# Output row of a decode kernel: four column groups of 112 columns on four partitions, one VectorE copy, a store from four partitions

## The chip, the cores and the metric

One core of a Trainium2 chip. The metric is the device time of one execution in microseconds (us); most executions of one kernel agree within about 0.9 us here, so medians of 3 to 9 runs are quoted. Before the change the median was 1276.21 us. Times inside an execution are counted from the start of its span; the span is about 1.3 us shorter than the timed execution.

## The reference, cut to what matters

One token goes through grouped attention over a cache of 65,536 positions and through a small gated feed-forward net; a gate mixes the two. Both halves end in a projection onto the same row of 448 numbers, so the kernel adds them in one accumulator.

```
q = x @ wq                                   # 448 -> 16 heads x 256
p = softmax(q k^T / 16);  o = p v            # k_cache, v_cache: 8 x 65536 x 256, bf16
a = o.reshape(1, 4096) @ wo                  # 4096 -> 448
h = relu(x @ W_gate) * (x @ W_up)            # 448 -> 1792
b = h @ W_down                               # 1792 -> 448
out = g * a + (1 - g) * b                    # row of 448, bf16 (896 B)
```

The two caches are 537 MB and have to be read once.

## The kernel before: what the change and the argument touch

The accumulator row lies in one PSUM tensor (the memory that the matmuls write), `A_ps` of 128 x 512 f32, as two halves of 224 columns on partitions 0 and 32. `proj` adds one contraction tile of 128 rows to it: two matmuls with a stationary operand of one column, in two column groups of the array. They run side by side: in the tail of the trace the two start 4 to 5 ns apart, and in a row the next pair starts 187 ns later, at a granted clock of 0.50.

```
D2 = D // 2                                   # 224
def proj(e, lhsT, rhs, start, stop):
    for g in range(2):
        ins = e.matmul(A_ps[32*g:32*g+1, 0:D2], lhsT, rhs[:, g*D2:(g+1)*D2], start=start, stop=stop,
                       skip_group_check=True, tile_position=(0, 32*g))
    return ins
# [...] down projection (ahead of the loop): 14 contraction tiles
def f_dn(e):
    for ft in range(FT):
        ins = proj(e, hT[:, ft:ft+1], wd_sb[:, ft, :], ft == 0, False)
# [...] output projection (after the loop): 8 heads x 4 tiles; weights come in five transfers, wo0 to wo4
def f_wo4(e, h=h):
    for s in range(4):
        ins = proj(e, attnT[:, h*4+s:h*4+s+1], wo4[:, h, s, :], False, False)
# [...] the end
fin_o = P_sb[0:1, 0:D]
f0 = op("dv", T_END, lambda e: e.tensor_copy(fin_o[:, 0:D2], A_ps[0:1, 0:D2]), [fin])
f1 = op("ac", T_END, lambda e: e.copy(fin_o[:, D2:D], A_ps[32:33, 0:D2]), [fin])
f2 = dma("sp", T_END + 1, "out", lambda e: e.dma_start(out[0, :, :], fin_o), [f0, f1])
```

TensorE's program has three pieces: code ahead of the loop over heads, the loop, and code after it (called the tail code here).

## Time and profile before

| | before |
|---|---|
| median of 3 runs | 1276.21 us (1276.04 to 1276.6) |
| span of the profiled execution | 1275.2 us |
| DMA traffic | 549 MB at 431 GB/s |
| matmuls into `A_ps` | 28 (down) + 64 (output), 224 columns each |

The kernel is bound by its transfers: the DMA engines are busy from first to last slice, no compute engine over half the time. Queue q8 carried 7 transfers of kind "instruction". It is 0.0% of the traffic.

The end of the chain of waits that ended last (start, duration, what):

```profile
1246.84 0.43 SPq L582
1247.28 0.04 issue
1247.32 23.46 DMA ring<-in_A_wo_dram
1270.78 0.04 issue
1270.82 0.91 PE A_ps L391 x8
1271.73 0.20 PE M_ps L426 x4
1271.93 1.67 PE A_ps L391 x15
1273.59 0.02 issue
1273.62 0.38 DVE P_sb L619
```

The timeline of the last 5 us (start, duration, engine, line, operation, output<-input, count, idle time before it and its releaser), then the wait of the store's queue:

```profile
1270.82 0.91 PE L391 MATMUL A_ps<-ring,attnT 128*1 128x224 bf16 x8 [0.73 <-DMA ring<-in_A_wo_dram]
...
1271.91 1.66 PE L391 MATMUL A_ps<-ring,attnT 128*1 128x224 bf16 x16
...
1273.04 0.09 PEld L391 LDWEIGHTS A_ps<-ring,attnT 128*1 128x1 bf16 x4 [0.29 <-DMA ring<-in_A_wo_dram]
1273.62 0.34 ACT L620 CAST P_sb<-A_ps 1x224 bf16<-1x224 f32 x1 [58.59 <-PE A_ps L391]
1273.62 0.38 DVE L619 CAST P_sb<-A_ps 1x224 bf16<-1x224 f32 x1 [1.49 <-PE A_ps L391]
1274.05 0.32 SPq L621 DMA_DIRECT2D out_dram<-P_sb  x1
```

```profile
SPq L644 <- DMA out_dram<-P_sb: 0.8, 1, 0.8
```

Read from the bottom: 0.8 us to the store's landing, 0.32 us to issue it, two copies side by side (the longer 0.38 us), and before them the last four matmuls, which a weight transfer released at 1273.04 us. Only this tail is not hidden under transfers. The matmul clock there is half speed, by windows (window, length, busy time of each engine and count, PEclk, DMA share, GB/s):

```profile
1271.00:1272.00 1.00, 1.00 (x14) 0.50 (x12) 0.04 (x1) 0.00 (x0) 0.00 (x0) 0.50 0.33 124
```

### The profile page before, as it was taken

How to read it: one execution, taken by the hardware profiler on the slowest of the kernel's cores; microseconds unless marked ns; L12 is line 12 of the kernel's file. 1: busy time of each engine (PE TensorE's matmuls, PEld its weight loads, DVE VectorE, ACT ScalarE, POOL GpSimd, SP SyncE). 2: the span in 40 equal slices, each digit the busy share in tenths (PEclk: the TensorE clock that was granted, in tenths of full speed). 3: DMA queues.
4: the chain of work that ended last, by engine and by line, in shares of the span. 5: the costliest groups of instructions: out<-in, count | busy, mean ns of one | idle time of the engine just before them, and what ended most of it. 6: DMA issues, size and time to landing. Idle time of an engine off the chain costs nothing. (4 is left out here: it accounts for less than half of the span.)

```text
span 1275.2 us, 10054 instructions
## 1 busy us (share of the span) xinstructions
PE 420.1 (33%) x4572; PEld 160.9 (13%) x4572; DVE 625.3 (49%) x240; ACT 63.3 (5%) x124; POOL 4.6 (0%) x21
## 2 busy tenths in 40 slices
PE   2423432334123432225331243322333324233235
PEld 1201110111001210012110111100111101011012
DVE  2697633465433655434555444555434655335600
ACT  0001000010000100001000010000100001000000
POOL 1000000000000000000000000000000000000000
PEclk8566666656566565666665666656666656666567
DMA  9999999999999999999999999999999999999998
GB/s 402 451 423 426 440 428 442 432 430 432 436 438 434 430 430 436 432 438 434 432 432 436 434 432 436 430 434 434 436 434 432 430 438 432 436 436 428 423 438 356
DMA packets 12050, 549.19 MB, mean 431 GB/s; under 512 B 1283, under 2 KB 1798, under 8 KB 3078
## 3 DMA queue, kind: packets, MB, share of 16 engines
q1 hardware_dynamic: 12034, 549.03, 99.7%
q8 instruction: 7, 0.11, 0.0%
q14 instruction: 5, 0.04, 0.0%
q10 hardware_dynamic: 4, 0.00, 0.0%
HBM read 549.03 MB, written 0.00 MB: 431 GB/s over the span
## 5 line engine op out<-in xcount | busy, mean ns | idle before, releaser
L369 DVE STREAM_TRANSPOSE ring<-ring 128x8192 uint32<-128x8192 uint32 x64 | 553.9, 8691 | 402.5 <-DMA ring<-in_A_k_cache_dram 402.5
L380 PE MATMUL ST<-ring,xc 128*16 128x512 bf16 x2048 | 223.8, 610 | 738.8 <-PEq L86 737.7
L380 PEld LDWEIGHTS ST<-ring,xc 128*16 128x16 bf16 x2048 | 68.4, 120 | 879.5 <-issue 877.3
L411 PE MATMUL O<-ring,ptp 128*4 128x512 bf16 x2048 | 150.2, 456 | 36.4 <-PEq L86 24.0
L521 ACT ACTIVATE P_sb<-ST,nmb 128x512 bf16<-128x512 f32 x32 | 45.2, 1412 | 1102.8 <-DVE nmb L519 1102.8
L519 DVE TENSOR_REDUCE nmb<-ST 128x1 f32<-128x512 f32 x32 | 22.0, 689 | 118.3 <-PE ST L380 118.3
L411 PEld LDWEIGHTS O<-ring,ptp 128*4 128x4 bf16 x2048 | 57.0, 100 | 129.7 <-issue 81.8
L421 DVE CAST o_sb<-O 128x512 bf16<-128x512 f32 x8 | 5.5, 691 | 77.5 <-PE O L411 77.5
L540 DVE TENSOR_TENSOR P_sb<-P_sb,hs 128x1024 bf16<-128x1024 bf16 x16 | 18.9, 1221 | 9.6 <-ACT hs L534 9.6
L545 PE MATMUL PT<-identb,P_sb 128*128 128x128 bf16 x128 | 16.2, 306 | 16.8 <-PEq L86 15.8
L545 PEld LDWEIGHTS PT<-identb,P_sb 128*128 128x128 bf16 x128 | 12.4, 138 | 19.2 <-issue 19.2
L554 ACT COPY ptp<-PT 128x256 bf16<-128x256 bf16 x32 | 10.3, 375 | 23.9 <-PE PT L545 23.9
L343 PE MATMUL QN<-ring,P_sb 128*128 128x512 bf16 x32 | 8.4, 429 | 3.9 <-DMA ring<-in_A_wq_dram 3.9
L521 ACT ACTIVATION_READ_ACCUMULATOR P_sb<-ST,nmb 128x1 f32 x32 | 8.4, 262 | 0.0
L478 PE MATMUL QN<-ring,xT 128*1 128x448 bf16 x16 | 1.7, 566 | 18.1 <-DMA ring<-in_B_W_up_dram 18.1
L433 PE MATMUL M_ps<-emat,o_sb 128*64 128x1 bf16 x112 | 4.5, 199 | 6.6 <-PEq L86 6.6
L458 DVE STREAM_TRANSPOSE scr<-P_sb 128x256 uint32<-128x256 uint32 x1 | 0.4, 445 | 12.7 <-ACT P_sb L457 12.7
L530 PE MATMUL M_ps<-identf,hs 128*2 128x128 f32 x8 | 2.6, 321 | 11.1 <-PEq L86 11.1
L440 DVE TENSOR_SCALAR attnT<-M_ps,hs 64x4 bf16<-64x4 f32 x14 | 3.1, 220 | 6.3 <-PE M_ps L433 6.2
L566 DVE RECIPROCAL hs<-M_ps 128x2 f32<-128x2 f32 x8 | 1.4, 170 | 8.3 <-PE M_ps L565 8.3
L433 PEld LDWEIGHTS M_ps<-emat,o_sb 128*64 128x64 bf16 x112 | 4.1, 154 | 9.9 <-issue 9.9
L391 PE MATMUL A_ps<-ring,attnT 128*1 128x224 bf16 x64 | 4.7, 305 | 1.3 <-DMA ring<-in_A_wo_dram 0.7
(80 smaller groups left out, 70.4 us busy)
## 6 DMA issues: line engine op xcount, KB each, us to landing
ring<-in_A_v_cache_dram SPq DMA_DIRECT2D x1, 4096.0 KB, 48.1
ring<-in_A_wq_dram SPq DMA_DIRECT2D x1, 3072.0 KB, 10.5
ring<-in_A_wo_dram SPq DMA_DIRECT2D x1, 2240.0 KB, 38.9
ring<-in_A_v_cache_dram SPq DMA_DIRECT2D x1, 2048.0 KB, 19.1
ring<-in_B_W_down_dram SPq DMA_DIRECT2D x1, 1568.0 KB, 22.8
ring<-in_B_W_gate_dram SPq DMA_DIRECT2D x1, 1344.0 KB, 32.6
ring<-in_B_W_up_dram SPq DMA_DIRECT2D x1, 1344.0 KB, 35.5
ring<-in_A_v_cache_dram SPq DMA_DIRECT2D x1, 1024.0 KB, 21.2
```

Source lines behind the costliest of these rows:

```text
L343: ins = e.matmul(QN_ps, xw3[:, k_, 31 - h:159 - h], rhs, start=(h == 0 and kt == 0), stop=(h == H - 1 and kt == R3))
L369: return lambda e: e.transpose(v, v)
L380: ins = e.matmul(bank[32 * w:32 * w + 16, :], xc[:, x0:x0 + 16], ktv[sl][:, u0:u0 + 16, c, :, r_], start=(b == 0 and c == 0 and r_ == 0), ...
L391: ins = e.matmul(A_ps[32 * g:32 * g + 1, 0:D2], lhsT, rhs[:, g * D2:(g + 1) * D2], start=start, stop=stop, skip_group_check=True, tile_pos ...
L411: ins = e.matmul(OP[32 * g:32 * g + 4, :], ptp[:, col:col + 13:4], ring[sl][:, base + k * 512:base + (k + 1) * 512], start=(a == 0 and k < ...
L421: o1 = op("dv", tn, lambda e: e.tensor_copy(o_sb[:], OP[:]), [pv[n], last.get(("otr", h - 1))])
L433: ins = e.matmul(T_ps[64 * q:64 * q + 64, s:s + 1], o_sb[:, par * 256 + s:par * 256 + 256:4], emat[:, 2 * par + q:2 * par + q + 1], start= ...
L519: smax[n] = op("dv", tk + 22, lambda e, n=n, NM=NM, t_=t_: e.tensor_reduce(NM[:, t_:t_ + 1], ST[n % 2][:], AX.X, ALU.max, negate=True), [q ...
L521: aexp[n] = op("ac", tk + 23, lambda e, n=n, t_=t_, NM=NM, RS=RS: e.activation(P_sb[:, t_:2048:4], ST[n % 2][:], ACTF.Exp, bias=NM[:, t_:t ...
L540: rsc = op("dv", tt, lambda e, X=X, pb=pb: e.tensor_tensor(pb, pb, X[:, 12:16].unsqueeze(1).to_broadcast([128, 256, 4]), ALU.mult), [h7, a ...
L545: ins = e.transpose(PT[rd][:, s * 128:(s + 1) * 128], P_sb[:, (rd * 8 + s) * 128:(rd * 8 + s + 1) * 128], identb[:, :])
L554: ins = e.copy(dst, src)
```

## The change

Its intent is to shorten the tail: four column groups at once instead of two, a copy half as wide on one engine, one wait fewer before the store. The new memset keeps the unused partitions of the copied block defined.

```
-        fin_o = P_sb[0:1, 0:D]
+        fin_o = P_sb[:, 0:D // 4]
 [...]
-        for i, tt in enumerate([ST[0], ST[1], OP]):
+        for i, tt in enumerate([ST[0], ST[1], OP, A_ps]):
             c_ps.append(op("dv", 0.04 + i * 0.001, lambda e, tt=tt: e.memset(tt[:], 0.0)))
 [...]
-        D2 = D // 2
+        D4 = D // 4
         def proj(e, lhsT, rhs, start, stop):
-            for g in range(2):
-                ins = e.matmul(A_ps[32 * g:32 * g + 1, 0:D2], lhsT, rhs[:, g * D2:(g + 1) * D2], ...
+            for g in range(4):
+                ins = e.matmul(A_ps[32 * g:32 * g + 1, 0:D4], lhsT, rhs[:, g * D4:(g + 1) * D4], ...
 [...]
-        f0 = op("dv", T_END, lambda e: e.tensor_copy(fin_o[:, 0:D2], A_ps[0:1, 0:D2]), [fin])
-        f1 = op("ac", T_END, lambda e: e.copy(fin_o[:, D2:D], A_ps[32:33, 0:D2]), [fin])
-        f2 = dma("sp", T_END + 1, "out", lambda e: e.dma_start(out[0, :, :], fin_o), [f0, f1])
+        f0 = op("dv", T_END, lambda e: e.tensor_copy(fin_o, A_ps[:, 0:D4]), [fin])
+        f2 = dma("sp", T_END + 1, "out", lambda e: e.dma_start(
+            out[0, :, :].rearrange("o (g d) -> (o g) d", g=4), fin_o[0:128:32, :]), [f0])
```

More of the change, by code (lines that the diff above doesn't have):

```diff
@@ L384, in f_qk @@
             return f
-        D2 = D // 2
+        D4 = D // 4
+        assert D % 4 == 0
         def proj(e, lhsT, rhs, start, stop):
-            for g in range(2):
-                ins = e.matmul(A_ps[32 * g:32 * g + 1, 0:D2], lhsT, rhs[:, g * D2:(g + 1) * D2], start=start, stop=stop,
+            for g in range(4):
+                ins = e.matmul(A_ps[32 * g:32 * g + 1, 0:D4], lhsT, rhs[:, g * D4:(g + 1) * D4], start=start, stop=stop,
                                skip_group_check=True, tile_position=(0, 32 * g))
@@ L503, in f_dn @@
                     return ins
-                l_["dn"] = op("pe", tg + 12.2, f_dn, [l_["hT"], a3])
+                l_["dn"] = op("pe", tg + 12.2, f_dn, [l_["hT"], a3, c_ps[3]])
                 assert tg + 12.2 < tL["k", 0] + 20
```

## The prediction

> **What bounds the kernel now.** HBM traffic. On the page the DMA engines are busy 9 tenths or more in all but the last of 40 slices, the hardware queue takes 99.7% of 16 engines' span, 431 GB/s for 549 MB. DVE is busy 49%, PE 33%. The chain of waits that ended last is one transfer of projection weights (23.5 us, to 1270.8 us) and about 4.4 us of tail. Only what lies in this tail, or what empties the DMA queue earlier, can move the time.
>
> **What the change touches.**
> 1. The projections into A_ps (down and output): each pair of matmuls over 224 columns becomes four over 112; by tile 28 + 64 matmuls become 56 + 128.
> 2. One more PSUM memset at the start on DVE (the present ones take 485 ns each).
> 3. The last copy: one DVE cast of 112 columns over 128 partitions instead of a DVE (379 ns) and an ACT cast (336 ns) of 224 columns side by side.
> 4. The store: four runs of 224 B from four partitions instead of one of 896 B.
>
> **Costs from the trace.** In the tail the granted clock is 0.50 (windows of 1 us, 1271 to 1275 us), and projection pairs start 187 ns apart (timeline, sixteen matmuls in 1.66 us): 224 columns at half clock, two column groups side by side. Four groups of 112 stream together in 93 ns, if issue keeps up. It should: the 16 one-column matmuls of the attention transpose, with their weight loads, take 0.65 us, 198 ns of it the last one's own duration: at most 30 ns each, 120 ns for four. [...] So about 100 to 120 ns per four instead of 187 per pair, and about 0.09 us less in the last matmul's own duration.
>
> On the critical path: the last weight piece lands near 1273.0 us and only four matmuls (0.53 us, to 1273.57) follow. They become eight in 0.35 to 0.4 us: gain 0.15 us. The down projection at 53 us gets about 1 us shorter, and the transfer that waits for it is issued earlier, but the queue isn't empty there: no gain. The first five heads' output projection at 1246 us (full clock, 52 ns a matmul) lies under transfers.
>
> Copy: 512 columns take 691 ns, 224 take 379, so 1.08 ns a column; 112 take about 260 ns: gain 0.12 us. ACT's copy wasn't the longer one.
>
> Memset: 0.49 us at about 4.1 us; the query projection waits for weights until 11.7 us, its DVE input is ready at 5.4 us: hidden.
>
> Store: today 0.32 us issue, 0.8 us to landing. [...] I allow 0 to 0.2 us more.
>
> **Sum:** -0.15 - 0.12 + 0.1, about -0.2 us: 1276.0 us, inside the spread of before's runs (0.56 us). Range 1275.0 to 1277.0. Faster by over 2%: 0.5%; within 2%: 98.5%; slower: 1%.
>
> **What would show it.** A_ps matmuls in the tail in fours within 100 to 120 ns at clock 0.50, own durations near 165 ns instead of 259; under 0.5 us from the last weight landing to the copy; copy near 260 ns; store wait 0.8 to 1.0 us; DMA share still 99%; query projection still from 11.7 us.
>
> **What would make it wrong.** If weight load plus matmul issue at 50 ns, four take 200 ns and the tail gains nothing. If four small stores take over 0.5 us more. If the earlier issue at 53 us reorders transfers so that a piece lands late at the end.

The sum: it came to -0.15 (matmuls) - 0.12 (copy) + 0.1 (store) = -0.17, about -0.2 us. But what is left for "about 100 to 120 ns per four" is the 93 ns of streaming and the at most 30 ns a matmul of the trace, and "0 to 0.2 us more" for the store, the source of the +0.1, is a guess of mine, drawn from no run.

## More of the kernel before

From the page of the kernel before (busy times; busy tenths of the DMA engines in 40 slices; DMA queues with packets, MB and share of 16 engines):

```profile
span 1275.2 us, 10054 instructions
PE 420.1 (33%) x4572; PEld 160.9 (13%) x4572; DVE 625.3 (49%) x240; ACT 63.3 (5%) x124; POOL 4.6 (0%) x21
...
DMA  9999999999999999999999999999999999999998
...
q1 hardware_dynamic: 12034, 549.03, 99.7%
q8 instruction: 7, 0.11, 0.0%
q14 instruction: 5, 0.04, 0.0%
```

The tail code is placed *ahead* of the loop in memory and skipped the first time:

```
pl.emit("pe", pe[:heads[0][0]], nc.tensor)                   # ahead of the loop
with nc.tensor.Fori(0, 2) as part:
    with nc.tensor.If_eq(part.val.handles[0], 1):
        pl.emit("pe", pe[end:], nc.tensor)                   # tail code, run in the second round
    with nc.tensor.If_eq(part.val.handles[0], 0):
        pl.emit_loop(H + 1, span, nc.tensor, go)             # the loop, run in the first round
```

## The result, and the profile after

| | before | after |
|---|---|---|
| median of 6 runs each | 1276.22 us (1275.99 to 1276.6) | 1277.36 us (1277.31 to 1277.63) |
| ratio after/before | | 1.0009 (95%: 0.9996 to 1.0022) |

Ratios are the mean time of one kernel's fast runs over that of the other's of the same rounds, so not quite the ratio of the medians. Executions over 1.5% slower than the fastest of the same kernel are left out of the means. The median lies 0.36 us above the top of the range, and by the medians the change cost 1.14 us where I had expected a gain of 0.2. No run of the one kernel overlaps the other's, so 0.1% or not, something systematic happened.

The same lines of the page after:

```profile
span 1276.0 us, 10237 instructions
PE 413.8 (32%) x4664; PEld 157.6 (12%) x4664; DVE 625.8 (49%) x241; ACT 63.1 (5%) x123; POOL 4.5 (0%) x21
...
DMA  9999999999999999999999999999999999999998
...
q1 hardware_dynamic: 12040, 549.03, 99.6%
q8 instruction: 9, 0.15, 0.0%
q14 instruction: 5, 0.04, 0.0%
```

The program has 92 more matmuls and 92 more weight loads, and q8 carried 9 instruction transfers instead of 7. The end of the chain, the timeline and the store's wait:

```profile
1249.67 23.92 DMA ring<-in_A_wo_dram
1273.59 0.04 issue
1273.64 0.38 PE A_ps L392 x8
1274.02 0.02 issue
1274.04 0.28 DVE P_sb L620
```

```profile
1272.50 0.94 PE L392 MATMUL A_ps<-ring,attnT 128*1 128x112 bf16 x24 [0.48 <-DMA ring<-in_A_wo_dram]
...
1273.64 0.36 PE L392 MATMUL A_ps<-ring,attnT 128*1 128x112 bf16 x8 [0.20 <-DMA ring<-in_A_wo_dram]
1274.04 0.28 DVE L620 CAST P_sb<-A_ps 128x112 bf16<-128x112 f32 x1 [1.82 <-PE A_ps L392]
1274.34 0.64 SPq L621 DMA_DIRECT2D out_dram<-P_sb  x1
```

```profile
SPq L645 <- DMA out_dram<-P_sb: 1.0, 1, 1.0
```

Walk the tail in both timelines. The last weights release TensorE at 1273.04 us before and 1273.64 after: **+0.6**. From there to the copy's start 0.58 and 0.40: **-0.18**. From the copy's start to the store's issue 0.43 and 0.30: **-0.13**. Issue 0.32 and 0.64, landing 0.8 and 1.0: **+0.5**. The sum is +0.8 us, the difference of the two spans. The profiled execution of before was one of the longer runs (1276.48 us, 0.26 above the median), so the typical difference of the landing is larger than 0.6, as the runs below show.

So the two gains came as predicted, the store cost more than I had allowed, and there is a term that the prediction didn't have at all: the last weights land later.

### The profile page after: what moved, and what is told of

It is laid out like the page before. It is cut to its first block, busy times and chain, and to the rows that moved or that the text cites. A ratio compares the mean times of both kernels' runs of the same rounds, so it can differ in the third digit from the quotient of the medians.

```text
span 1276.0 us, 10237 instructions
## 1 busy us (share of the span) xinstructions
PE 413.8 (32%) x4664; PEld 157.6 (12%) x4664; DVE 625.8 (49%) x241; ACT 63.1 (5%) x123; POOL 4.5 (0%) x21
## 5 line engine op out<-in xcount | busy, mean ns | idle before, releaser
L412 PE MATMUL O<-ring,ptp 128*4 128x512 bf16 x2048 | 147.4, 450 | 36.2 <-PEq L86 23.7
L533 PE MATMUL M_ps<-mx,nselT 2*128 2x1 f32 x16 | 3.4, 279 | 4.1 <-PEq L86 4.1
```

The costliest lines, as they stand in the source:

```text
L412: ins = e.matmul(OP[32 * g:32 * g + 4, :], ptp[:, col:col + 13:4], ring[sl][:, base + k * 512:base + (k + 1) * 512], start=(a == 0 and k < ...
L533: h5 = mop("pe", T + 15, lambda e, h=h: e.matmul(NMR_ps, nselT[0:2, :], mx2[0:2, 0:1], start=True, stop=True), [h4, l_["ns"]])
```

## The experiments

**Theory A**, which the runs below are to test: TensorE's longer program no longer fits in what it can hold. Near the end it fetches two 16 KB blocks of instructions, through the same DMA engines that carry the data. Each fetch delays one of the 16 engines, and the last weights are complete only when the slowest engine has delivered. The trace has q8's packets, of 16,384 B each, with their times: before, all 7 lie between 54 and 107 us. After, 7 lie there and two more start at 1251.86 us (lasting 1.06 us) and 1263.24 us (1.09 us). I take q8 to be TensorE's because its packets change where only TensorE's program does: in the five padded kernels below there are 7 to 11 of them, while q14 keeps its 5. **Rival B.** The last group of transfers was issued 0.65 us later (1246.18 us against 1245.52), because TensorE happened to be at half clock for longer just before (PEclk from 1240 to 1244 us 0.50, in before 0.59): late issue, late landing. **Rival C.** The new shapes or the memset.

Here is the evidence that ties A to the landing, from the trace. Every large transfer has 16 landings (wo4's lie from 1270.44 to 1273.00 us before), as many as the page counts DMA engines. The landings carry no engine number, only times. That each is the landing of one engine is my reading, and "an engine" below means one of the 16 in this reading; that they keep their distances from transfer to transfer, as shown below, agrees with it. The last three landings of three transfers:

```
                                             before                      after
the cache tile (8 MB) due at 1260       1258.86 1259.12 1259.72     1259.19 1259.33 1259.77
the 2 MB piece after it                 1263.75 1264.02 1264.61     1264.09 1264.21 1264.67
wo4, the fifth transfer of weights      1272.16 1272.40 1273.00     1272.61 1273.02 1273.59
```

The slowest engine is within 0.06 us of before until 1264.7 us and then 0.6 us later: just the transfers behind the fetch of 1263.24 us. All 16 landings, compared from the 2 MB piece to the transfer after it, show how: fifteen move on by the same 2.48 us to within 0.04, and one falls behind them by about 1.5 us, more than the 1.09 us that the fetch itself lasted. That engine was not the last before (it would have landed at about 1266.2 us and landed at 1267.71), and from there on it is the last. The fetch of 1251.86 us also set one engine back by 1.5 us, but one that was 2.5 us ahead of the last, and cost nothing. In each experiment below, "last landing" is the last of wo4's 16.

### TensorE's program made longer, nothing else: pad_before

The kernel before plus 92 one-column matmuls into an unused corner of `A_ps`, 28 beside the down projection and 64 in the tail code, at a time when transfers hide them.

```
+        def dummy(e, lhsT, rhs, n):
+            for _ in range(n):
+                ins = e.matmul(A_ps[64:65, 256:257], lhsT, rhs[:, 0:1], start=True, stop=True, ..., tile_position=(0, 64))
 [...] in f_dn:   + ins = dummy(e, hT[:, ft:ft + 1], wd_sb[:, ft, :], 2)
 [...] in f_wo4:  + if h < 4: ins = dummy(e, attnT[:, ...], wo4[:, h, s, :], 4)
```

> The kernel before plus 92 one-column matmuls that nobody reads (28 beside the down projection, 64 under the transfers at 1246 us), so that TensorE's program is as long as after the change; copy and store as before. Theory A (the longer program makes TensorE fetch two more 16 KB blocks of instructions near the end, and each fetch takes a slice of one DMA engine, so the last weights land later): the instruction queue shows 9 transfers instead of 7, two of them after 1250 us, last weight landing about 0.6 us later, time +0.5 to +1.0 us on the kernel before. Rival B (the final transfers are issued 0.65 us later because the half-clock phase fell differently): no change beyond 0.3 us. Rival C (the shapes of the matmuls or the extra memset): no change.

Measured: 1277.15 us (1276.98 to 1277.38) against 1276.00 (1275.84 to 1276.07) for before on the same chip; ratio 1.0009. Its queue line, and its end with before's own copy and store:

```profile
q8 instruction: 9, 0.15, 0.0%
```

```profile
1274.21 0.38 DVE L628 CAST P_sb<-A_ps 1x224 bf16<-1x224 f32 x1 [1.45 <-PE A_ps L391]
1274.64 0.32 SPq L630 DMA_DIRECT2D out_dram<-P_sb  x1
```

Fetches at 1249.51 and 1255.91 us, last landing at 1273.59 us. Instructions that compute nothing cost 1.15 us, as much as the whole change (+1.14) and a little more than expected. Rivals B and C are not needed for it. In this trace one engine lands the cache tile at 1260.31 us, 1.2 us behind the second slowest, and stays 1.2 us behind to the end: a lag handed on unchanged for 13 us. TensorE itself also stands for 2.3 us up to 1251.86 us here, which I read as a wait for instructions, but that is over 8 us before the cache tile lands.

### The change with the program made short again: trim_after

Half of the down projection's tiles and four heads' output projection are left out, so the result is wrong; the number of TensorE instructions is that of before in both places.

```
 in f_dn:  - for ft in range(FT):   + for ft in range(FT // 2):
 [...] in the loop over heads of the output projection:
           + if h < 4: continue
```

> After the change, with half of the down projection's contraction tiles and four of the first five heads' output projection left out, so that TensorE's program is as long as before the change (wrong result on purpose; tail, copy and store as after). Theory A: no instruction fetch after 1250 us, 7 in all; the landing of the last weights is back at the kernel before's, time 0.5 to 1.0 us below the changed kernel: about 1276.2 to 1276.8, that is +0.1 to +0.4 us on before for the store. Rivals B and C: time stays at about 1277.4.

Measured: 1276.18 us (1276.08 to 1276.34), before 1276.00 on the same chip. The page shows:

```profile
q8 instruction: 7, 0.11, 0.0%
```

No late fetch, last landing 1272.57 us, and the time is 1.2 us below the changed kernel's 1277.36, which was measured in another call (by the difference to before in the same call, 0.96 us below). What remains, +0.18 us by the medians, is the change without its side effect: -0.18 - 0.13 + 0.5 = +0.2. Even then it doesn't gain, because of the store.

### The last group of transfers issued later: late_issue

Before, with the first of these transfers made to wait for the fourth head's output projection.

```
+                if h == 3:
+                    vp_dma[1].deps.append(fin)
```

> The kernel before, but the last group of transfers is issued only after the output projection of the fourth head, about 2 us later than now (1247.5 instead of 1245.5 us), while the transfer ahead of it still runs until 1260 us. Theory A: the queue is not empty, so no change (within 0.3 us of before). Rival B (late issue makes late landing): +0.6 us or more, up to +2 us.

Measured: 1275.95 us (1275.87 to 1275.97), before 1276.00; the group was issued at 1247.26 us, 1.7 us later than before's; last landing 1272.47 us, no late fetch. Rival B falls: a group issued 1.7 us later landed no later. The transfer ahead of it was still under way (before's cache tile has its last landing at 1259.72 us). This run also shows what before's landing can be. Its profiled execution (1273.00) had one engine trailing; here, and in the two runs padded ahead of the loop below, it is 1272.47 us. Against that, 1273.59 us is +1.1 us. Over all profiles without a late fetch the landing lies between 1272.47 and 1273.00 us (before_split4 below: 1272.83), and over those with a loss between 1273.59 and 1273.72. In all 14 profiles the timed execution is 3.5 to 3.8 us longer than the last landing, so the landing and the 0.2 us by which the change lengthens what follows it nearly account for the time.

### The store alone: after_row_store

After, but the four groups are copied into one row, two by VectorE and two by ScalarE, and stored as one run.

```
+        fin_o = P_sb[0:1, 0:D]
+        copy g: fin_o[:, g * D4:(g + 1) * D4] <- A_ps[32 * g:32 * g + 1, 0:D4]   # g = 0, 1 VectorE; 2, 3 ScalarE
+        f2 = dma(..., e.dma_start(out[0, :, :], fin_o), [f0, f1])
```

> After the change, but the four column groups are copied into one row on one partition (two copies on VectorE, two on ScalarE, side by side) and stored as one run of 896 B. Isolates the store: the profile of after shows 0.64 us issue and 1.0 us landing against 0.32 and 0.8. Expected: issue 0.32, landing 0.8, copies 0.5 to 0.6 us instead of 0.28; time 0.1 to 0.3 us below the changed kernel, with the late landing kept (9 fetches).

Measured: 1276.94 us (1276.91 to 1277.08), before 1276.00 on the same chip. Its end:

```profile
1274.04 0.50 ACT L623 CAST P_sb<-A_ps 1x112 bf16<-1x112 f32 x2 [60.13 <-PE A_ps L392]
1274.04 0.54 DVE L623 CAST P_sb<-A_ps 1x112 bf16<-1x112 f32 x2 [1.65 <-PE A_ps L392]
1274.64 0.32 SPq L628 DMA_DIRECT2D out_dram<-P_sb  x1
```

```profile
SPq L651 <- DMA out_dram<-P_sb: 0.8, 1, 0.8
```

The copy starts at 1274.04 us in both this kernel and after; from there to the end of the span it is 1.8 us here and 2.0 after. Issue and landing are back at before's, so the four-partition store costs 0.5 us, and the four small copies that avoid it cost 0.3 us. By the median the kernel is 0.94 us over before, where the change was 1.14 and 1.51 us over it. They were run at other times. The last landing stays late (1273.59 us; 10 fetches, of which the two at 1249.46 and 1262.61 us precede it).

### The changed kernel again, and more or less padding: after_again, pad_head, pad_tail, pad_double, pad_head92

The first four ran on one chip. Edits to pad_before's `dummy` counts: pad_head has only the 28 ahead of the loop, pad_tail only the 64 in the tail code, pad_double 28 and 192. pad_head92, run later, has 92 ahead of the loop and none in the tail code:

```
 pad_double:  in f_wo4  - dummy(..., 4)   + dummy(..., 12)
 pad_head92:  in f_dn   - dummy(..., 2)   + dummy(..., 8 if ft < 4 else 6)      and none in f_wo4
```

> The changed kernel unaltered, as the reference of this call. Theory A: +1.0 to +1.3 us on before, two instruction fetches after 1245 us, last weight landing near 1273.9 us.

> The kernel before plus only the 28 idle matmuls (with weight loads 56 instructions) beside the down projection, ahead of the loop. Theory A in the form that the whole program's length decides: one late fetch or none, time +0 to +0.6 us. Theory A in the form that only the code after the loop decides: no late fetch, no change.

> The kernel before plus only the 64 idle matmuls after the loop (128 instructions[...]). Theory A: at least one late fetch, time +0.5 to +1.2 us. If it stays at before's time with no late fetch, the threshold lies between 64 and 92 matmuls.

> The kernel before plus 220 idle matmuls (28 ahead of the loop, 192 after it): 128 more than in the first padded kernel[...]. Theory A: one fetch more than there (10 in all, three late); each fetch holds one DMA engine for about 1.1 us, so +1.1 to +2.3 us on before, by whether it falls to the engine that is already last. A rival in which the padding costs through TensorE's own time: [...] the time stays as in the first padded kernel (+1.15 us).

> The kernel before plus 92 idle matmuls, all beside the down projection, ahead of the loop: the whole program as long as after the change, the code after the loop as short as before. If the whole program's length decides: a late fetch and +1.1 us. If only the code that has to stay loaded from the tail on decides: no late fetch, time within 0.4 us of before.

| kernel | extra matmuls ahead of loop + in tail code | median us | before | fetches in all; starts after 1200 us | last two landings of wo4 |
|---|---|---|---|---|---|
| after_again | (the change: 28 + 64) | 1277.51 | 1276.00 | 9; 1249.45, 1263.25 | 1272.42, 1273.61 |
| pad_head | 28 + 0 | 1276.36 | 1276.00 | 7; none | 1272.24, 1272.47 |
| pad_tail | 0 + 64 | 1277.35 | 1276.00 | 10; 1251.20, 1274.86 | 1272.78, 1273.72 |
| pad_double | 28 + 192 | 1277.16 | 1276.00 | 11; 1249.47, 1255.99, 1262.13, 1273.84 | 1273.66, 1273.72 |
| pad_head92 | 92 + 0 | 1276.13 | 1276.10 | 8; none | 1272.30, 1272.47 |

Four things follow. First, the length of the whole program does not decide, so theory A's first sentence fails in that form: 92 matmuls ahead of the loop bring one more fetch, but an early one (all eight lie between 54 and 107 us), and no loss by the median (1275.99 to 1277.22; the one run at 1277.22 has no trace and is not explained). What counts is the tail code. Second, one fetch is enough: in pad_tail just one precedes the last landing, and the last engine is late by 1.2 us against pad_head92. There TensorE's branch back to the tail code also stood for 7.7 us, from 1245.80 us (0.2 us in before, from 1245.47), with the fetch of 1251.20 us inside that time; transfers hid this. Third, pad_double shows that the cost is per engine, not a sum: two engines are late together (1273.66 and 1273.72 us), the time is that of one. The number of fetches was one above my expectation, an estimate whose ground is cut, and the cost was at the bottom of the range given for theory A; the time alone (+1.16 us) would have fitted the rival named there as well, the landings and pad_before decide against it. Fourth, in after_again the first fetch leaves the cache tile's last landing at 1259.16 us and only the second makes an engine trail the others: the fetch on an engine that is ahead cost nothing. pad_head's +0.36 us is not covered by its last landing, which equals that of pad_head92; its runs (1276.11 to 1276.54) overlap those of before (1275.90 to 1276.51), and the profiled one was at 1276.11.

### The tail code placed behind the loop: after_tail_last

```
-        with nc.tensor.Fori(0, 2) as part:
-            with nc.tensor.If_eq(part.val.handles[0], 1):
-                pl.emit("pe", pe[end:], nc.tensor)
-            with nc.tensor.If_eq(part.val.handles[0], 0):
-                pl.emit_loop(H + 1, span, nc.tensor, go)
+        pl.emit_loop(H + 1, span, nc.tensor, go)
+        pl.emit("pe", pe[end:], nc.tensor)
```

> The changed kernel with TensorE's code after the loop placed behind the loop in the program, instead of ahead of it. If fetching runs ahead far enough, its blocks are loaded early with the rest and no fetch falls after 1240 us: about 0.9 to 1.1 us below the changed kernel, 1276.2 to 1276.5. If fetching waits until the loop ends: several late fetches, time as the changed kernel or up to 2 us longer.

Measured: 1276.26 us (1276.11 to 1276.65), before 1276.10 on the same chip; the result is right. The time is as expected, but not for the reason that I gave: fetches do fall late, at 1251.86 and 1270.80 us. The first, like the first in the changed kernel, set back by 1.5 us an engine that was 2.4 us ahead of the last one. The second comes 7.6 us later than the changed kernel's second and leaves the landings of the last weights in step. So no engine trails (last two landings 1272.89 and 1272.93 us). All five runs were near before's time. Why this placement fetches its second block so late is not settled.

### Four runs from one partition: before_split4

```
-  e.dma_start(out[0, :, :], fin_o)
+  e.dma_start(out[0, :, :].rearrange("o (g d) -> o g d", g=4), fin_o.rearrange("o (g d) -> o g d", g=4))
```

> The kernel before, with the row on its one partition stored as four runs of 224 B. If the four runs cost it: issue 0.64 us and 1.0 us to landing as after the change, +0.5 us. If it is the four partitions: 0.32 and 0.8 us, no change.

Measured: 1275.93 us, before 1276.10; issue 0.32 us, landing 0.8 us. The trace shows why this tells nothing: the store still went out as one packet of 896 B (12,050 packets in all, as before), not as four. Whether it is the four packets or the four partitions that cost 0.5 us is open.

### Both repairs on the change: tail_last_row

The edits of after_tail_last and after_row_store together.

> Both repairs on the changed kernel: TensorE's code after the loop placed behind the loop, and the row put together on one partition and stored as one run. If the terms add up (the late fetch no longer on the last engine -1.1 us, store -0.5 us, copies +0.3 us): 1275.9 to 1276.2, level with the kernel before within 0.2 us, so the quicker matmuls (0.17 us) are then just spent on the four copies. If it beats before by over 0.3 us a term is mis-sized; if it is over 0.4 us slower, a fetch falls on the last engine again.

Measured: 1276.16 us (1275.87 to 1276.31), before 1276.22 on the same chip (eight runs, 1275.85 to 1276.63; one run of 1327 us left out); ratio 0.9999. Two fetches fall late, at 1252.03 and 1270.44 us, and neither makes an engine trail. The terms add up: last landing 1272.56 us, 0.45 us from there to the copies, copies 0.54, issue 0.32, landing 0.8. A correct kernel with the quicker matmuls is level with before, and does not beat it.

## Why the prediction was right and wrong

- *Right: transfers bind, and only the tail can move the time.* DMA share 9 tenths in all slices but the last, both times.
- *Right: the matmuls, "gain 0.15 us".* The last matmuls and their wait took 0.58 us before and 0.40 after. The eight took 0.36 us, within the 0.35 to 0.4 given. The last one's own duration fell from 391 to 298 ns, by the 0.09 us that I had said. My 259 and 165 ns were at fault all the same: 259 is the duration at full clock (PEclk 1.00), at 1246 us, where it fell to 213, and the tail runs at half clock (0.50). In a longer row, fours of matmuls start 92 to 93 ns apart there, less than the 100 to 120 given. Issue keeps up: at full clock, from 1246.84 us, 80 of them, each with its weight load, start 12 ns apart in the mean ((1.16 - 0.21) us / 79).
- *Right: the copy, "112 take about 260 ns: gain 0.12 us".* 275 ns; 0.13 us up to the store's issue.
- *Right: the memset is hidden.* It takes 485 ns at 4.2 us, the query projection still starts at 11.65 us.
- *Mis-sized: the store, "I allow 0 to 0.2 us more".* It is +0.5 us: issue doubled from 0.32 to 0.64 us, which I had not put in the sum at all, and the landing rose from 0.8 to 1.0. I had looked at the small runs; the trace shows the four packets of 224 B at 14 to 15 ns each, the one of 896 B at 41 ns. The packets are not where the time is: from the start of the issue to the first packet it is 0.75 us before and 1.24 after, from the end of the last data packet to the end of the wait 0.33 and 0.32.
- *Wrong: "the last weight piece lands near 1273.0 us and only four matmuls follow", taken as fixed by the change.* This is the step that failed, and by 1.1 us it decided the result: the landing moved to 1273.59 us, from 1272.47 where nothing trails (1273.00 in the profiled run of before). Under "what would make it wrong" I had a piece landing late, but through the earlier issue at 53 us. What the runs showed in its place is, by my reading of the landings, an instruction fetch on the DMA engine that ends up last: padding that computes nothing brings the loss (+1.15), trimming takes it away (+0.18 left), a later issue does nothing (-0.05).

The sum with the measured terms, by the profiles: +1.1 (landing) - 0.18 (matmuls) - 0.13 (copy) + 0.5 (store) = +1.3 us. The timed differences are +1.14 and +1.51 us.

I could have looked for it. The profile counted the 7 blocks. The trace of before shows them all fetched by 107.7 us and none after that, over the rounds of the loop and the branch back to the tail code at 1245.47 us (0.2 us); so nothing was fetched late there. The tail code's odd place ahead of the loop may have been a hint that somebody had already met this. How much TensorE can hold, and so how much room was left before the change, no run here shows; what was loaded before the traced span is not known either. The exact rule, how much tail code may be added before a fetch falls late, is not settled: 64 matmuls were too many, and none, with 92 ahead of the loop, was harmless.

## What to carry to other kernels

Count instructions as a cost of a change even where the engine is idle. This kernel is bound by transfers, and 64 or 92 matmuls that compute nothing made it 1.35 us (pad_tail) and 1.15 us (pad_before) longer where the tail code grew: instruction fetches fell late, and a fetch of 1.09 us (after) set one of 16 landings back by about 1.5 us, which was the last one from there on (1273.59 us, against 1272.47 where none trails). Compare the instruction queue's transfers and their times before and after any unrolling, above all near the end: the lag of 1.2 us in pad_before was handed on unchanged for 13 us, to the last landing. And price the issue of a store, not only its bytes: splitting one run of 896 B over four partitions cost 0.5 us here (issue 0.64 us against 0.32, landing 1.0 against 0.8), more than the 0.13 us that a copy half as wide gained.
